# Batch-2 loads and weight stores ordered behind the raw weight loads on SyncE, and two weight conversions moved between softmax sums, in a fused attention and cos-FFN kernel

## The chip, the cores and the metric

The kernel runs on one core of one Trainium2 chip. The metric is the time of one execution on the device in microseconds (us); less is better. Before the change three runs took 944.4, 944.38 and 940.06 us, median 944.38.

## What is computed

Attention with two kinds of masks, followed by a feed-forward layer whose activation is h·cos(h). All inputs are float32.

```
def _attn_ref(q, k, v):                      # (8, 8, 576, 64): batch, heads, positions, head size
    scores = scale * np.matmul(q, k.transpose(0, 1, 3, 2))
    mask_local = (rel >= 0) & (rel < 32)                     # heads 0 to 3
    mask_strided = (rel >= 0) & (pos[None, :] % 32 == pos[:, None] % 32)   # heads 4 to 7
    attn = softmax(np.where(masks, scores, -1e9))
    return np.matmul(attn, v)

def _moe_ref(x, w_in, w_out):                # x (4608, 512), w_in (512, 2048), w_out (2048, 512)
    h = x @ w_in
    g = h * np.cos(h)
    return g @ w_out
```

## The kernel before

The 4608 tokens are worked through in 12 blocks `j` of 384. The hidden width of 2048 is cut into 16 slices `f` of 128. A **chunk** (j, f) is `hidden`: 12 matmuls of 384 columns into PSUM bank a or b (L467), the curve h·cos(h) on ACT and DVE (L473, L474, L477, L480), and a split of the result into a high part on ACT (L483) and a rest on POOL (L484). `outer` follows three chunks later (`LAG`): 9 matmuls of 512 columns into the output's accumulators (L491). High and low parts exist because each float32 operand is multiplied in two parts.

Blocks 0 to 5 (`PLAIN`) are done in this way, blocks 6 to 11 in pairs by a scheme with seven products for eight (L757 and L786), which reads sums and copies of the weights back from DRAM, `wis` and `wos`.

Attention is cut into seven **units** a batch: four strided ones (L360 for scores) and three local ones (L305). A unit is: scores on PE; a softmax that goes back and forth between DVE (maximum L249, subtraction L250, sum L272, L273, reciprocal L274), ACT (exponent L261) and POOL (product L276); then either three transposes on PE (L380, strided) or one on DVE (L314, local); the products with v (L394 or L329); and a copy to x by ACT. The 14 units of batches 0 and 1 come ahead of the feed-forward ("plain"), with an Exp; the 42 units of batches 2 to 7 lie between the chunks of blocks 2 to 5, with two Silu and a Square (L265, L266, L270) in place of Exp, a subtraction on POOL (L256), and ACT's copy L384 between the transposes L380 and the products. The curve's Sin needs another table on ACT than Exp, so the first L477 has a table load ahead of it.

The **weights** come as float64 in memory. `load_weight` (L140 and below) loads one raw tile of 512 KB on SP's queue (L144; three buffers) and converts it to float32 parts: on DVE L158 (or on ACT L153, for `w_out`), L161 and L167, on ACT L166 and the cast L171, on POOL the rest L172. `need_weights` (L176) does this for `w_in` and `w_out` of slice f. A converted slice's first DVE operation is ordered behind the curve's L474 of chunk (0, f - 2): `after = reduced[f - AHEAD]`. For f = 0 and 1 there is no such order, and they are converted among the softmaxes of batches 0 and 1; f = 2 and up follow among the chunks. Raw tile number n is ordered behind load number 4 + n of the attention's q and k.

`put_away` (L584) stores parts of the converted weights to `wis` (L589) and `wos` (L597), also on SP's queue. The later units' loads of q and k (L295, L345) and of v (L291, L349) stand on the same queue.

The program text gives no final order: a scheduler puts each engine's instructions in an order by a simulated time, kept within the explicit `order(later, first, ...)` calls. Each engine and each queue then works strictly in that order.

Of the kernel before, what the change touches and what calls it, by code (L numbers as in the profile page):

```python
# [13 lines left out]
F32 = mybir.dt.float32  # L14
# [5 lines left out]
ALU = mybir.AluOpType  # L20
AX = mybir.AxisListType

B, H, S, D = 8, 8, 576, 64
# [22 lines left out]
VL = (LU + 1) * D  # L46
QS, KS, VS = SU * GB, SU * GB, SU * D
# [7 lines left out]

LAG = 3
AHEAD = 2

WEIGHTS_AT, WEIGHTS_EACH = 4, 1

# [26 lines left out]
def attention_cos_ffn(ctx, tc, qkl, vl, qkvs, w_in, w_out, eye, eye16, mask_l0, mask_l, mask_s, out):  # L87
    nc = tc.nc
# [21 lines left out]
    pn_s = [const.tile([P, SU, GP], F32, name=f"pn_s{i}") for i in range(2)]  # L110
    for t in pn_s:
        nc.gpsimd.memset(t, 0.0)
    exps, reduced, loads, tiles = [], [], [], []

    def half(n, rows=64):
        return slice(64 * n, 64 * n + rows)
# [4 lines left out]
    def order(later, first, reason):  # L121
        tc.add_manual_dep(
            later.ins, first.ins.name,
            mybir.DependencyInfo(mybir.DependencyClass.NoSync, mybir.DependencyReason.DATA), reason=reason,
        )
# [11 lines left out]
    wis = [dram.tile([7, P, 2, 2 * P], F32, name=f"wis{q}") for q in range(NQ)]  # L137
    wos = [dram.tile([P, 2, DM], F32, name=f"wos{f}") for f in range(NFC)]
# [35 lines left out]
    weights = 0  # L174

    def need_weights(cv, f):  # L176
        nonlocal weights
        for f in range(weights, f + 1):
            after = reduced[f - AHEAD] if 0 <= f - AHEAD < len(reduced) else None
            load_weight(  # L180
                cv, w_in.bitcast(I32)[f], wi_h[f].rearrange("p c n -> p (c n)"),
                wi_l[f].rearrange("p c n -> p (c n)"), after, False,
            )
            load_weight(cv, w_out.bitcast(I32)[f], wo_h[f], wo_l[f], after, True)
            weights = f + 1
# [16 lines left out]
    class Attention:  # L202
# [42 lines left out]
        def softmax(self, s, mask, n, w, pn=None):  # L245
            t = self.wk.tile([P, SC], F32, name="t_sb", bufs=3 if self.plain else 2)[:, :n * w].rearrange("p (t w) -> p t w", w=w)
            mx = sm.tile([P, SU], F32, name="mx")
            if self.plain:
                nc.vector.tensor_reduce(out=mx[:, :n], in_=s, op=ALU.max, axis=AX.X)  # L249
                nc.vector.tensor_tensor(  # L250
                    out=t, in0=s, in1=mx[:, :n].unsqueeze(2).broadcast_to([P, n, w]), op=ALU.subtract
                )
            else:
                nc.vector.tensor_tensor(out=t, in0=s, in1=mask, op=ALU.add)
                nc.vector.tensor_reduce(out=mx[:, :n], in_=t, op=ALU.max, axis=AX.X)
                nc.gpsimd.tensor_tensor(  # L256
                    out=t, in0=t, in1=mx[:, :n].unsqueeze(2).broadcast_to([P, n, w]), op=ALU.subtract
                )
            if self.plain:
                e = t  # L260
                exps.append(nc.scalar.activation(out=e, in_=t, func=AF.Exp, scale=0.125))  # L261
            else:
                e = self.wk.tile([P, SC], F32, name="e_sb", bufs=3)
                e = e[:, :n * w].rearrange("p (t w) -> p t w", w=w)
                nc.scalar.activation(out=e, in_=t, func=AF.Silu, bias=shift1, scale=0.0625)  # L265
                nc.scalar.activation(out=t, in_=t, func=AF.Silu, bias=shift2, scale=0.0625)  # L266
                nc.vector.scalar_tensor_tensor(
                    out=e, in0=t, scalar=-math.exp(STEP), in1=e, op0=ALU.mult, op1=ALU.add
                )
                nc.scalar.activation(out=e, in_=e, func=AF.Square, scale=math.exp(SHIFT) / STEP)  # L270
            z = sm.tile([P, SU], F32, name="z")
            nc.vector.tensor_reduce(out=z[:, :n], in_=e, op=ALU.add, axis=AX.X)  # L272
            nc.vector.tensor_scalar(out=z[:, :n], in0=z[:, :n], scalar1=1e-9, scalar2=None, op0=ALU.add)  # L273
            nc.vector.reciprocal(out=z[:, :n], in_=z[:, :n])  # L274
            pn = e if pn is None else pn
            nc.gpsimd.tensor_tensor(  # L276
                out=pn, in0=e, in1=z[:, :n].unsqueeze(2).broadcast_to([P, n, w]), op=ALU.mult
            )
            return pn
# [7 lines left out]
        def local(self, b, u):  # L287

            def load_v():
                v = self.ld.tile([P, max(VL, VS)], F32, name="v", bufs=5 if self.plain else 3)  # L290
                nc.sync.dma_start(out=v[:, :VL], in_=vl[b, u])  # L291
                return v

            qk = self.ld.tile([P, max(QKL, QS + KS)], F32, name="qk")
            loads.append(nc.sync.dma_start(out=qk[:, :QKL], in_=qkl[b, u]))  # L295
            if self.plain:
                v = load_v()
            q_t = qk[:, :2 * LQ].rearrange("p (h q) -> p h q", h=2)
            k_t = qk[:, 2 * LQ:QKL].rearrange("p (h k) -> p h k", h=2)
            mask = ml0.rearrange("p (t w) -> p t w", w=KW) if u == 0 else ml.unsqueeze(1).broadcast_to([P, LU, KW])  # L300
            s_ps = self.score_bank(mask)

            def score(t, c):
                p, j = divmod(c, 2)
                self.scored = self.pe(nc.tensor.matmul(  # L305
                    s_ps[quarter_of(c), t * KW:(t + 1) * KW], q_t[half(j), p, QB * t:QB * (t + 1)],
                    k_t[half(j), p, QB * t:QB * t + KW], start=not self.plain, stop=True, skip_group_check=True,
                ))

            yield [partial(score, t, c) for t in range(LU) for c in range(LH)], "64x32"  # L310
            pn = self.softmax(s_ps[:, :LU * KW].rearrange("p (t w) -> p t w", w=KW), mask, LU, KW)

            pt = self.wk.tile([P, LU * KW], F32, name="pt_l", bufs=2 if self.plain else 3)
            nc.vector.transpose(out=pt[:, :LU * KW], in_=pn.rearrange("p t w -> p (t w)"))  # L314
            yield
            if not self.plain:
                v = load_v()
            v_t = v[:, :VL].rearrange("p (m d) -> p m d", d=D)
            yield
            x_t = [self.wk.tile([P, LQ], F32, name="x_l") for _ in range(2)]  # L320
            a_ps = [self.bank(self.products), self.bank(self.transposed)]

            def product(m, c):


                p, j = divmod(c, 2)
                lo, hi = max(m - 1, 0), min(m + 1, LU)
                at = m * KW - QB if m else 0
                self.pe(nc.tensor.matmul(  # L329
                    a_ps[p][half(j), lo * QB:hi * QB], v_t[quarter_of(c), m], pt[quarter_of(c), at:at + (hi - lo) * QB],  # L330
                    start=m == turns[0], stop=m == turns[-1], skip_group_check=True,
                ))


            turns = range(0 if u else 1, LU + 1)
            yield [partial(product, m, c) for m in turns for c in range(LH)], "32x64"
            nc.scalar.copy(out=x_t[0], in_=a_ps[0][:, :LQ])
            nc.scalar.copy(out=x_t[1], in_=a_ps[1][:, :LQ])
            for p in range(2):
                keep(2 + p, b * S + u * LQ, x_t[p])  # L340

        def strided(self, b, p, u):
            real = min(SU, NG - SU * u)
            qk = self.ld.tile([P, max(QKL, QS + KS)], F32, name="qk")
            loads.append(nc.sync.dma_start(out=qk[:, :QS + KS], in_=qkvs[b, p, u, :, :QS + KS]))  # L345

            def load_v():
                v = self.ld.tile([P, max(VL, VS)], F32, name="v", bufs=5 if self.plain else 3)
                nc.sync.dma_start(out=v[:, :real * D], in_=qkvs[b, p, u, :, QS + KS:QS + KS + real * D])  # L349
                return v  # L350

            if self.plain:
                v = load_v()
# [21 lines left out]
            if not self.plain:  # L375
                v = load_v()
# [29 lines left out]
            if full < real:  # L406
                left = STRIDE % GR
                nc.scalar.copy(
                    out=x_v[:, :, STRIDE - left:],
# [173 lines left out]

    def put_away():  # L584

        for q in range(NQ):
            for i, f, k in ((1, q, 0), (2, q, 1), (5, q + NQ, 1)):
                for part, w in enumerate((wi_h, wi_l)):
                    nc.sync.dma_start(  # L589
                        out=wis[q][i][:, part],  # L590
                        in_=w[f][:, 2 * k:2 * k + 2].bitcast(F32).rearrange("p c n -> p (c n)"),
                    )
                if i != 2:
                    yield
            for f in (q, q + NQ):
                for part, w in enumerate((wo_h, wo_l)):
                    nc.sync.dma_start(out=wos[f][:, part], in_=w[f].bitcast(F32))  # L597
                yield

    direct = {j: x_operands() for j in range(2)}  # L600
# [349 lines left out]
```

## Time and profile before

| | |
|---|---|
| three timed runs | 944.4, 944.38, 940.06 us |
| profiled execution | 939.62 us, its span 937.8 us |
| PE busy | 903.8 us, 96% of the span |
| DVE, ACT, POOL busy | 527.8, 519.8, 436.4 us |
| PE idle from 45 to 60, 60 to 80 us | 5.54, 2.16 us |
| PE idle from 80 to 260 us | 0 us |
| PE idle from 260 to 500 us | 14.8 us |
| DMA moved | 166.33 MB, mean 177 GB/s |

The span is the time from the first to the last instruction; the execution's time has 1.8 us around it. The units of batches 0 and 1 end, and the chunks begin, near 55 us; batch 2 begins near 200 us, the paired blocks near 500 us. PE's busy time by itself says little, since a matmul's end is modelled and overlaps the next one's start; where consecutive matmuls start at steady distances (0.174 us for 384 columns, 0.229 us for 512) PE is full.

In the quoted rows of a timeline the columns are the start and the duration in us, the engine, line, operation, the output and its inputs, the shapes, how many instructions in a row are merged, and in brackets the idle time ahead of it on this engine and what ended it. Rows of waits give the total, the number of times and the longest in us.

### The profile page before, as it was taken

Reading aid. Unit: us, or ns where it says so; the run is one execution under the profiler, and the core shown is the slowest. Engines: PE = TensorE matmul, PEld = TensorE weight load, DVE = VectorE, ACT = ScalarE, POOL = GpSimd, SP = SyncE. Lnnn points to the kernel's source line nnn. Section 1 sums busy time; section 2 is a strip of 40 time slices with the busy share of each in tenths; the row PEclk is TensorE's granted clock in tenths of the full one; section 3 lists DMA queues with packets and bytes.
Section 4 is the critical chain, followed back from the end, with each engine's and each line's share of the span. In section 5 each row is a group of like instructions: output and inputs, shape, how many; then the busy total and the mean of one; then the engine's idle time right before and its main releaser. Section 6 shows DMA issues by size and latency. Waiting matters only on the chain.

```text
span 937.8 us, 20557 instructions
## 1 busy us (share of the span) xinstructions
PE 903.8 (96%) x7876; PEld 793.2 (85%) x7876; DVE 527.8 (56%) x1018; ACT 519.8 (55%) x1090; POOL 436.4 (47%) x466
## 2 busy tenths in 40 slices
PE   8879999999999997999999999999999999999998
PEld 4668899998888886888878889898998889999996
DVE  5758756446657555665654334646456464545453
ACT  3556777466666555665565544545555455544443
POOL 2636665535655566555745522535325444223231
PEclk9799999999999999999999999999999999999999
DMA  8938866222245534544354856666676565756401
GB/s 287 317 116 290 281 227 215 94 100 86 92 154 184 172 120 155 172 148 129 121 203 135 273 159 190 202 195 202 199 247 215 185 196 162 253 186 208 136 23 67
DMA packets 93265, 166.33 MB, mean 177 GB/s; under 512 B 10736, under 2 KB 34032, under 8 KB 93168
## 3 DMA queue, kind: packets, MB, share of 16 engines
q1 hardware_dynamic: 85248, 157.72, 52.0%
q10 hardware_dynamic: 7920, 7.31, 2.3%
q8 instruction: 62, 1.02, 0.5%
q14 instruction: 35, 0.29, 0.1%
HBM read 125.40 MB, written 39.58 MB: 176 GB/s over the span
## 4 chain that ended last, share of the span: by engine, by line
PE 43%; POOL 10%; DVE 7%; ACT 7%; issue 5%; DMA 1%; ACTq 0%; POOLq 0%; DVEq 0%
PE acc L786 18%; PE a L757 10%; PE b L757 7%; PE acc L491 4%; POOL g_lo L484 3%; POOL t_sb L256 2%; PE b L467 2%; PE a L467 2%; POOL wf L559 2%; POOL sr L567 1%; DVE r L480 1%; ACT e_sb L265 1%; DVE r L766 1%; DVE r L768 1%; POOL pn_s L276 1%
## 5 line engine op out<-in xcount | busy, mean ns | idle before, releaser
L772 POOL TENSOR_TENSOR g_lo<-r,g_hi 128x384 fp32r<-128x384 f32 x96 | 101.9, 1061 | 246.2 <-ACT g_hi L771 141.3
L484 POOL TENSOR_TENSOR g_lo<-r,g_hi 128x384 fp32r<-128x384 f32 x96 | 102.8, 1070 | 167.9 <-ACT g_hi L483 96.0
L491 PE MATMUL acc<-s,g_hi 128*128 128x512 f32 x576 | 180.0, 396 | 0.0
L786 PE MATMUL acc<-s,g_hi 128*128 128x512 f32 x576 | 179.7, 393 | 0.0
L491 PEld LDWEIGHTS acc<-s,g_hi 128*128 128x128 f32 x576 | 105.3, 188 | 15.5
L786 PEld LDWEIGHTS acc<-s,g_hi 128*128 128x128 f32 x576 | 106.2, 188 | 10.8
L786 PE MATMUL acc<-s,g_lo 128*128 128x512 f32 x288 | 112.8, 392 | 0.0
L766 DVE SCALAR_TENSOR_TENSOR r<-r,h 128x384 f32<-128x384 int32 x96 | 64.0, 667 | 85.5 <-ACT r L765 85.5
L491 PE MATMUL acc<-s,g_lo 128*128 128x512 f32 x288 | 110.9, 390 | 0.0
L467 PE MATMUL b<-x_hi,s 128*128 128x384 f32 x384 | 109.5, 346 | 1.1 <-DVE r L480 1.1
L467 PE MATMUL a<-x_hi,s 128*128 128x384 f32 x384 | 109.5, 346 | 1.0 <-DVE r L480 1.0
L757 PE MATMUL a<-s,s 128*128 128x384 f32 x384 | 83.1, 337 | 0.0
L767 ACT ACTIVATE r<-r,biases 128x384 f32<-128x384 f32 x96 | 59.2, 617 | 42.5 <-DVE r L766 42.4
L768 DVE TENSOR_TENSOR r<-r,h 128x384 f32<-128x384 f32 x96 | 64.5, 671 | 23.6 <-ACT r L767 21.6
L477 ACT ACTIVATE r<-r,biases 128x384 f32<-128x384 f32 x96 | 58.9, 614 | 30.8 <-DVE r L474 29.1
L765 ACT ACTIVATE r<-h 128x384 int32<-128x384 f32 x96 | 50.3, 524 | 45.0 <-DVE h L835 29.4
L467 PEld LDWEIGHTS b<-x_hi,s 128*128 128x128 f32 x384 | 71.0, 190 | 4.6 <-DVE r L480 1.9
L467 PEld LDWEIGHTS a<-x_hi,s 128*128 128x128 f32 x384 | 70.6, 189 | 4.0 <-DVE r L480 1.4
L757 PEld LDWEIGHTS a<-s,s 128*128 128x128 f32 x384 | 69.3, 188 | 4.2
L771 ACT CAST g_hi<-r 128x384 fp32r<-128x384 f32 x96 | 49.1, 512 | 42.0 <-DVE r L768 41.9
L483 ACT CAST g_hi<-r 128x384 fp32r<-128x384 f32 x96 | 49.0, 511 | 34.6 <-DVE r L480 33.7
L467 PE MATMUL b<-x_lo,s 128*128 128x384 f32 x192 | 64.8, 338 | 0.0
(141 smaller groups left out, 1764.6 us busy)
## 6 DMA issues: line engine op xcount, KB each, us to landing
s<-wis SPq DMA_DIRECT2D x168, 256.0 KB, 2.9
s<-wos SPq DMA_DIRECT2D x96, 256.0 KB, 3.5
qk<-in_qkvs SPq DMA_DIRECT2D x32, 324.0 KB, 3.6
qk<-in_qkl SPq DMA_DIRECT2D x24, 416.0 KB, 3.9
out<-o SPq DMA_DIRECT2D x36, 256.0 KB, 2.6
raw<-in_w_in SPq DMA_DIRECT2D x16, 512.0 KB, 5.4
raw<-in_w_out SPq DMA_DIRECT2D x16, 512.0 KB, 3.9
wos<-s SPq DMA_DIRECT2D x32, 256.0 KB, 5.1
```

Of the source, the lines that this page charges most:

```text
L467: mm = nc.tensor.matmul(h, w[f][:, c], x[c], start=(i == 0), stop=(i == len(ops) - 1))
L477: sin = nc.scalar.activation(out=r, in_=r, func=AF.Sin, bias=quarter)
L484: chain["rest"] = nc.gpsimd.tensor_tensor(out=g_lo, in0=r, in1=g_hi.bitcast(F32), op=ALU.subtract)
L491: mm = nc.tensor.matmul(acc[t], g[:, ts], w[f], start=(f == 0 and i == 0), stop=(f == NFC - 1 and i == 2))
L757: in_turn(nc.tensor.matmul(bank, w[:, n, c], part, start=start and i == 0, stop=stop and i == len(ops) - 1, skip_group_check=True,))
L765: nc.scalar.activation(out=k, in_=h, func=AF.Copy, scale=1.0 / (2.0 * math.pi), bias=0.25)
L766: nc.vector.scalar_tensor_tensor(out=r, in0=k, scalar=-2.0 * math.pi, in1=h, op0=ALU.mult, op1=ALU.add)
L767: nc.scalar.activation(out=r, in_=r, func=AF.Sin, bias=quarter)
L768: chain["curve"] = nc.vector.tensor_tensor(out=r, in0=r, in1=h, op=ALU.mult)
L771: chain["cast"] = nc.scalar.copy(out=g_hi, in_=r)
L772: chain["rest"] = nc.gpsimd.tensor_tensor(out=g_lo, in0=r, in1=g_hi.bitcast(F32), op=ALU.subtract)
L786: in_turn(nc.tensor.matmul(acc, g[gn][:, ts], w[wn], start=done == 0 and i == 0, stop=done == NFC - 1 and i == 2,))
```

## The change

Three things are done.

- All loads of units that are not plain (batches 2 to 7) are ordered behind the last raw load, `tiles[-1]`.
- All stores of `put_away` are ordered behind the last unit load that the program has named at that point, `loads[-1]`. So they too stand behind the raw loads.
- Slices f = 2 and 3 are converted behind the softmax sum (L272) number 10 and 13 of the plain units, counted from 0, in place of the curves of chunks (0, 0) and (0, 1). Sums 10 and 13 belong to the eleventh and the last of the 14 plain units.

```diff
 LAG = 3
 AHEAD = 2
+CONVERTED = {2: 10, 3: 13}
...
-            after = reduced[f - AHEAD] if 0 <= f - AHEAD < len(reduced) else None
+            after = summed[CONVERTED[f]] if f in CONVERTED else reduced[f - AHEAD] if f >= AHEAD else None
...
-            nc.vector.tensor_reduce(out=z[:, :n], in_=e, op=ALU.add, axis=AX.X)
+            summed.append(nc.vector.tensor_reduce(out=z[:, :n], in_=e, op=ALU.add, axis=AX.X))
...
             loads.append(nc.sync.dma_start(out=qk[:, :QKL], in_=qkl[b, u]))
+            if not self.plain:
+                order(loads[-1], tiles[-1], "weights first")
...
-                nc.sync.dma_start(out=v[:, :VL], in_=vl[b, u])
+                load = nc.sync.dma_start(out=v[:, :VL], in_=vl[b, u])
+                if not self.plain:
+                    order(load, tiles[-1], "weights first")
...
+        def put(out, part):
+            order(nc.sync.dma_start(out=out, in_=part), loads[-1], "units first")
+
         for q in range(NQ):
...
-                    nc.sync.dma_start(
-                        out=wis[q][i][:, part],
-                        in_=w[f][:, 2 * k:2 * k + 2].bitcast(F32).rearrange("p c n -> p (c n)"),
-                    )
+                    put(wis[q][i][:, part], w[f][:, 2 * k:2 * k + 2].bitcast(F32).rearrange("p c n -> p (c n)"))
...
-                    nc.sync.dma_start(out=wos[f][:, part], in_=w[f].bitcast(F32))
+                    put(wos[f][:, part], w[f].bitcast(F32))
```

No instruction is added or taken away on an engine. In the changed file the lines are numbered one to nine higher (L158 is L159 there, L161 L162, L167 L168, L172 L173, L249 L250, L272 L273, L274 L275, L384 L393, L473 L482).

**DVE and POOL at the end of the plain units.** On DVE, from the sum of unit 10 to the sum of unit 11; before:

```order
L272 TENSOR_REDUCE z<-t_sb 128x6
L273 TENSOR_SCALAR z<-z 128x6
L274 RECIPROCAL z<-z 128x6
L249 TENSOR_REDUCE mx<-acc_851 128x6
L250 TENSOR_TENSOR t_sb<-acc_851,mx 128x324
L272 TENSOR_REDUCE z<-t_sb 128x6
```

and in the changed kernel, where `bits` and `raw` are the tiles of a weight's conversion:

```order
L273 TENSOR_REDUCE z<-t_sb 128x6
L159 TENSOR_SCALAR bits<-raw 128x512
L274 TENSOR_SCALAR z<-z 128x6
L162 SCALAR_TENSOR_TENSOR bits<-raw,bits 128x512
L162 SCALAR_TENSOR_TENSOR bits<-raw,bits 128x512
L275 RECIPROCAL z<-z 128x6
L250 TENSOR_REDUCE mx<-acc_851 128x6
L168 SCALAR_TENSOR_TENSOR bits<-raw,bits 128x512
L251 TENSOR_TENSOR t_sb<-acc_851,mx 128x324
L168 SCALAR_TENSOR_TENSOR bits<-raw,bits 128x512
L273 TENSOR_REDUCE z<-t_sb 128x6
```

The five DVE operations of f = 2 stand between the steps of two softmaxes; the same five of f = 3 stand in the same manner around the last unit's reciprocal. On POOL, from the product of unit 10 (`pn_s_85`) to that of unit 12, the changed kernel has

```order
L277 TENSOR_TENSOR pn_s_85<-t_sb,z 128x6x54
L173 TENSOR_TENSOR s_142<-bits,s_126 128x512
L173 TENSOR_TENSOR s_110<-bits,s_94 128x512
L277 TENSOR_TENSOR pn_s_86<-t_sb,z 128x6x54
L435 TENSOR_TENSOR x_lo<-x_l,x_hi 128x192 x2
L277 TENSOR_TENSOR t_sb<-t_sb,z 128x384
```

where before the two rests of the weights, now ahead of unit 11's product `pn_s_86`, stood behind the first chunk's L484.

**SP's queue.** Behind the raw load of `w_out` for f = 1, before:

```order
L144 DMA raw<-in_w_out 128x1024
L291 DMA v<-in_vl 128x448
L589 DMA wis_160<-s_92 128x256 x2
L291 DMA v<-in_vl 128x448
L345 DMA qk<-in_qkvs 128x648
L589 DMA wis_160<-s_108 128x256
L144 DMA raw<-in_w_in 128x1024
L589 DMA wis_160<-s_108 128x256
L597 DMA wos_168<-s_124 128x512
```

In the changed kernel those stores are gone from there and the first of them stand behind the last raw load, between the first loads of batch 2:

```order
L145 DMA raw<-in_w_out 128x1024
L350 DMA qk<-in_qkvs 128x648
L596 DMA wis_160<-s_92 128x256
L596 DMA wis_160<-s_108 128x256
L350 DMA qk<-in_qkvs 128x648
```

**ACT among the later units.** The scheduler also gave ACT, DVE and POOL another order at a number of places from batch 2 on, with PE's order there unchanged. One of them on ACT, before, around the copy `pt<-acc_3103`:

```order
L473 ACTIVATE r<-b 128x384
L265 ACTIVATE e_sb<-t_sb,biases 128x384
L384 COPY pt<-acc_3103 128x324
L266 ACTIVATE t_sb<-t_sb,biases 128x384
L477 ACTIVATE r<-r,biases 128x384
```

and in the changed kernel:

```order
L266 ACTIVATE e_sb<-t_sb,biases 128x384
L267 ACTIVATE t_sb<-t_sb,biases 128x384
L482 ACTIVATE r<-b 128x384
L393 COPY pt<-acc_3103 128x324
L271 ACTIVATE e_sb<-e_sb 128x384
L486 ACTIVATE r<-r,biases 128x384
```

The copy now stands behind both Silu of the next unit's softmax and the chunk's L473.

More of the change, by code (lines that the diff above doesn't have):

```diff
@@ L112, in attention_cos_ffn @@
         nc.gpsimd.memset(t, 0.0)
-    exps, reduced, loads, tiles = [], [], [], []
+    exps, summed, reduced, loads, tiles = [], [], [], [], []
     def half(n, rows=64):
@@ L345, in strided @@
             loads.append(nc.sync.dma_start(out=qk[:, :QS + KS], in_=qkvs[b, p, u, :, :QS + KS]))
+            if not self.plain:
+                order(loads[-1], tiles[-1], "weights first")
             def load_v():
                 v = self.ld.tile([P, max(VL, VS)], F32, name="v", bufs=5 if self.plain else 3)
-                nc.sync.dma_start(out=v[:, :real * D], in_=qkvs[b, p, u, :, QS + KS:QS + KS + real * D])
+                load = nc.sync.dma_start(out=v[:, :real * D], in_=qkvs[b, p, u, :, QS + KS:QS + KS + real * D])
+                if not self.plain:
+                    order(load, tiles[-1], "weights first")
                 return v
```

## The prediction, made blind

> **What bounds the kernel now.** I read the page's span first, then a table of busy time by stretches of the span, because the share of 96% for PE is an average over very different stages.
>
> ```profile
> span 937.8 us, 20557 instructions
> core 0: us, PE busy (x) PEld busy (x) DVE busy (x) ACT busy (x) POOL busy (x), PEclk, DMA share, GB/s
> 18.00:45.00 27.00, 22.95 (x525) 17.19 (x524) 20.97 (x48) 15.84 (x43) 18.81 (x22) 0.75 0.96 319
> 45.00:60.00 15.00, 9.46 (x310) 7.65 (x299) 7.79 (x21) 6.38 (x21) 5.33 (x8) 0.98 0.20 65
> 60.00:80.00 20.00, 17.84 (x85) 16.05 (x84) 14.85 (x22) 13.99 (x26) 9.14 (x7) 0.93 0.78 250
> 80.00:180.00 100.00, 100.00 (x505) 90.82 (x504) 62.34 (x107) 70.87 (x132) 59.45 (x49) 1.00 0.67 223
> 180.00:260.00 80.00, 80.00 (x868) 70.62 (x867) 46.56 (x102) 48.76 (x104) 42.05 (x50) 1.00 0.30 97
> 260.00:500.00 240.00, 225.21 (x3110) 195.48 (x3109) 146.22 (x329) 141.32 (x327) 139.99 (x174) 0.99 0.47 152
> ```
>
> From 80 to 260 us PE is never idle: 100.00 of 100 and 80.00 of 80. Most of the stores that the change moves, and the DMA queues that are 0.67 busy there, cost PE nothing in that stretch. PE has something to lose or to win in three places only: ahead of 45 us (clock 0.75, DMA 0.96), from 45 to 80 (5.5 and 2.2 us idle), and from 260 to 500 (14.8 us idle). The list of what PE waited for after 60 us is headed by the third.
>
> ```profile
> PE acc L329 <- ACT pt L384: 9.2, 5, 2.8
> PE acc L380 <- ACT x_l L338: 5.2, 4, 2.2
> ```
>
> No row of that list names a DMA. The other waits of weight in it are two on r, of 1.0 and 1.1 us, whose rows stand further down; it is only through these that a late raw load of weights reaches PE.
>
> **Conversion of f = 2 and 3, moved ahead.** Prices first, from the timeline of DVE and POOL where f = 2 is converted now:
>
> ```profile
> 62.82 0.42 DVE L158 TENSOR_SCALAR bits<-raw 128x512 int32<-128x512 int32 x1
> 63.15 1.29 DVE L161 SCALAR_TENSOR_TENSOR bits<-raw,bits 128x512 int32<-128x512 int32 x2
> 66.47 0.69 DVE L167 SCALAR_TENSOR_TENSOR bits<-raw,bits 128x512 int32<-128x512 int32 x1
> 68.00 2.56 POOL L172 TENSOR_TENSOR s<-bits,s 128x512 fp32r<-128x512 f32 x2
> ```
>
> One f is 0.42 + 1.29 + 2 x 0.64 = 3.0 us of DVE and 2.56 us of POOL. These now stand inside the softmax chains of the last four units of batch 1, where each step waits for the one ahead:
>
> ```profile
> 49.11 0.73 POOL L276 TENSOR_TENSOR pn_s<-t_sb,z 128x324 f32<-128x324 f32 x1 [1.08 <-DVE z L274]
> 52.04 0.83 POOL L276 TENSOR_TENSOR t_sb<-t_sb,z 128x384 f32<-128x384 f32 x1 [1.10 <-DVE z L274]
> 53.41 0.52 DVE L249 TENSOR_REDUCE mx<-b 128x6 f32<-128x384 f32 x1
> 57.34 0.58 DVE L314 STREAM_TRANSPOSE pt_l<-t_sb 128x384 f32<-128x384 f32 x1 [1.19 <-POOL t_sb L276]
> 58.33 1.02 PE L329 MATMUL acc<-pt_l,v 32*64 32x32 f32 x56 [2.65 <-DVE pt_l L314]
> ```
>
> Unit 10's reciprocal gets L158 and two L161 ahead of it, 1.7 us. On POOL both L172 of f = 2 stand ahead of unit 11's pn_s (49.11). They wait for ACT's two casts, the second of which waits for the second L167; adding the durations up I get the casts done at about 51.1, pn_s at 52.5, and after it the two x_lo of POOL's row, so that unit 12's product (52.04) starts at about 54.35, 2.3 late. Its transpose, and behind it on DVE unit 13's maximum (53.41), are as late. Unit 13's own reciprocal then gets f = 3's L158 and two L161 ahead of it, 1.7 more; its two L167 lie in the wait for POOL (1.19). So the last L329 comes about 4.0 us later than 58.33.
>
> That is without waits between DVE and POOL, and the trace shows such waits earlier, where the same operations ran beside POOL:
>
> ```profile
> 19.91 1.27 POOL L172 TENSOR_TENSOR s<-bits,s 128x512 fp32r<-128x512 f32 x1
> 20.51 1.23 DVE L167 SCALAR_TENSOR_TENSOR bits<-raw,bits 128x512 int32<-128x512 int32 x1
> 23.10 1.26 POOL L172 TENSOR_TENSOR s<-bits,s 128x512 fp32r<-128x512 f32 x1
> 23.40 1.25 DVE L158 TENSOR_SCALAR bits<-raw 128x512 int32<-128x512 int32 x1
> ```
>
> L158 takes 1.25 us there and 0.42 alone; L167 1.23 and 0.64; both end about when POOL's operation does. Two such meetings add 0.6 + 0.8 = 1.4 us, so the last L329 is 4.0 to 5.4 us late. [...]
>
> What comes back is behind that L329:
>
> ```profile
> 59.37 0.32 ACT L337 COPY x_l<-acc 128x192 f32<-128x192 f32 x1 [2.89 <-PE acc L329]
> 59.72 0.81 ACTq L459 DMA_DIRECT2D xT<-x_l  x2
> 61.82 0.49 ACT L473 ACTIVATE r<-a 128x384 int32<-128x384 f32 x1 [1.91 <-PE a L467]
> 62.90 1.28 ACT L477 ACT_TABLE_LOAD   x1
> 64.19 0.62 ACT L477 ACTIVATE r<-r,biases 128x384 f32<-128x384 f32 x1
> 65.45 0.44 PE L467 MATMUL a<-x_hi,s 128*128 128x384 f32 x1 [1.04 <-DVE r L480]
> 71.85 0.68 ACT L153 ACTIVATE bits<-raw 128x512 int32<-128x512 uint32 x1 [1.97 <-DMA raw<-in_w_out]
> 79.31 0.44 PE L467 MATMUL b<-x_hi,s 128*128 128x384 f32 x1 [1.12 <-DVE r L480]
> ```
>
> Now 6.1 us pass from the end of L329 (58.33 + 1.02) to the third chunk's start (65.45), and on ACT an L153 (0.68, as at 71.85) stands between L473 and the table load. In the changed order PE does the whole first chunk of L467 and three matmuls of the second ahead of L329, so ACT's L473 can follow the two copies at once: copies 0.5, L473 0.5, two DMA issues 0.8, table load 1.3, L477 0.6, L480 0.55, starts 0.15: 4.4 us, with no L153 between. That is 1.7 us back. From 65.45 to 79.31 are 13.9 us; the 36 matmuls of 384 columns (starts 0.174 apart in this stretch) and 27 of 512 (0.229) need 12.4. The difference of 1.4 goes, because f = 3, whose L153 sat on ACT's queue for 1.97 us until its raw tile landed, is done by then. Sum: +4.0 - 1.7 - 1.4 = **+0.9 us** without the waits at POOL, +2.3 with them; I take the middle, **+1.6**. The bounds: if f = 2 hides wholly in the idle time of that stretch, only f = 3's 1.7 is left and 1.7 - 3.1 = -1.4; if another stretch of half clock falls behind the longer gap ahead of L329 and into dense work, it costs half of some 3.4 us more, +2.3 + 1.7 = +4. The profile has one such stretch behind the gap of 2.65 us; it is what brings the clock from 60 to 80 us to 0.93 (7% of 20 us lost is 1.4, near that half of 3.4). [...]
>
> **Loads and stores on SP.** Removed from 18 to 180 us: 80 stores of weights, now behind the last raw load.
>
> ```profile
> q1 hardware_dynamic: 85248, 157.72, 52.0%
> wos<-s SPq DMA_DIRECT2D x32, 256.0 KB, 5.1
> wis<-s SPq DMA_DIRECT2D x48, 128.0 KB, 4.9
> qk<-in_qkvs SPq DMA_DIRECT2D x32, 324.0 KB, 3.6
> ```
>
> They are 14.7 MB, by q1's row 14.7 / 157.72 x 52% x 937.8 = 45 us of all 16 engines. Between 180 and 300 us they raise a share of 0.30 to about 0.7. SP spends 0.33 us on each issue, and waits most of its time there anyway. Unit loads stand among them with two buffers, some 11 us ahead of their use against 3.6 us to landing; even 5.1 fits. I take **0**; with the cover gone, a load late by 1.5 us at one unit in eight of 42 costs +8. Ahead of 45 us the relief can help: PE stalled at 23.58 without a releaser, the clock then fell, and slow matmuls stand ahead of DVE's wait at 39.87.
>
> ```profile
> 23.58 0.49 PE L305 MATMUL a<-qk 64*32 64x64 f32 x18 [1.71 <-issue]
> 34.97 3.19 PE L329 MATMUL acc<-pt_l,v 32*64 32x32 f32 x100 [1.17 <-ACT x_t L402]
> ```
>
> At full clock the 100 matmuls and the six behind them take 2 us less. Bounds -2 and 0; I take 0, since DVE is busy without a pause up to 35 us and keeps its order.
>
> **Order on ACT, 240 to 500 us.** The scheduler put the two L265/L266 of the next softmax ahead of the copy L384 at five places (at 241, 271, 292, 372 and 394 us). What this does is seen where it is so already:
>
> ```profile
> 364.16 0.61 ACT L265 ACTIVATE e_sb<-t_sb,biases 128x384 f32<-128x384 f32 x1 [3.79 <-POOL t_sb L256]
> 365.70 0.42 ACT L384 COPY pt<-acc 128x324 f32<-128x324 f32 x1
> 366.17 1.37 PE L329 MATMUL acc<-pt_l,v 32*64 32x32 f32 x52 [2.82 <-ACT pt L384]
> ```
>
> ACT stood still for 3.79 us for POOL with L384 queued behind. Of ten copies in that order now, four made PE wait. Five more, each later by L266 and L473 (0.5 + 0.4), give 0 to +4.5; two places go the other way, -2 if they heal waits. I take **+2.0**.
>
> **Sum.** +1.6 + 0 + 2.0 = +3.6 us on the profiled execution's 939.62 (span 937.8 and 1.8 around it): 943.2. The four executions shown (939.62, 940.06, 944.38, 944.4) have their middle at 942.2, 2.6 above the profiled one; so **945.8 us**.
>
> **Rivals.** (1) *DMA relief decides.* The stall at 23.58 goes, the clock stays up (-2), f = 2 hides (-1.4 in place of +1.6), and no copy gets later (0 in place of +2): 945.8 - 7 = 938.8. For it: a DMA share of 0.96 in the very stretch where stores leave. Against it: no row shows DVE, which sets the pace there, waiting for a load or a store. (2) *ACT's head of queue decides, slower.* At all five places ACT comes to L265 before POOL is ready and PE waits 1.9 us each (9.2 / 5), 9.5 in place of 2.0: 953.3 us; with late unit loads behind the stores up to 955. It decides from the point at which POOL's L256 ends more than the 0.9 us after L384's input. For it: POOL is the one whom ACT waits for at 364. Against it: six of ten such copies cost nothing. (3) *The stores and raw loads were never in each other's way* and the conversion is a wash: 942.2 to 944.4, no change.
>
> **How the numbers follow.** Chances: forecast 0.47, rival 1 0.25, rival 2 0.19, rival 3 0.09. A measurement of this kernel can tell about 0.5% (4.7 us) from no change. Faster by more: 0.19 of rival 1 and 0.03 of the forecast's edge, 0.22. Slower by more: all of rival 2 and 0.07 of the forecast, 0.26. Within: 0.52. The range reaches from 937 (rival 1 and a spread of 2) to 955 (rival 2).
>
> **What would show it.** In the changed profile: the last L329 ahead of the first curve near 62 to 64 us; the first L480 some 3.8 us after it; no wait near 79 us, and PE full from about 70 us. Between 180 and 300 us a DMA share near 0.7 with no PE wait on a DMA. From 260 to 500 one or two more waits on L384. I am wrong if the sixth chunk starts ahead of 79 us, if PE's clock stays at 1.00 from 25 to 39 us, or if PE's idle time from 260 to 500 changes by over 5 us.

## The result, and the profile after

| | before | after |
|---|---|---|
| timed runs | 944.4, 944.38, 940.06, 941.98 | 953.51, 953.87, 952.84, 954.27 |
| median, us | 943.18 | 953.69 |
| ratio, 95% interval | 1 | 1.0116 [1.0087, 1.0145] |
| profiled execution, us | 939.62 | 953.51 |

The kernel became 1.2% slower: 10.5 us between the medians, 13.9 us between the two profiled executions. The time lies inside the predicted range (937 to 955). But I had called "no change" the likeliest, at 945.8, and the loss is three times the +3.6 of my sum.

Stretches of the changed kernel, with the columns of the table before (busy time and instructions of PE, its weight loads, DVE, ACT and POOL; the granted clock; the DMA share; GB/s):

```profile
span 951.7 us, 20514 instructions
25.00:39.00 14.00, 9.41 (x195) 7.22 (x198) 10.56 (x26) 9.19 (x25) 11.26 (x14) 0.76 0.65 212
45.00:60.00 15.00, 10.26 (x254) 8.10 (x245) 11.89 (x27) 9.05 (x23) 6.86 (x9) 0.89 0.30 105
60.00:80.00 20.00, 13.89 (x101) 12.53 (x100) 6.55 (x12) 9.45 (x18) 7.44 (x7) 0.66 0.27 83
80.00:180.00 100.00, 100.00 (x505) 91.08 (x505) 58.46 (x108) 71.82 (x132) 56.65 (x48) 1.00 0.37 131
180.00:260.00 80.00, 80.00 (x770) 70.65 (x770) 42.47 (x93) 45.65 (x95) 36.49 (x43) 1.00 0.46 146
260.00:500.00 240.00, 223.55 (x3077) 193.83 (x3079) 140.29 (x322) 138.62 (x324) 140.00 (x175) 0.97 0.57 187
```

PE is still full from 80 to 260 us, and the DMA queues are relieved as intended (0.37 in place of 0.67 from 80 to 180). Two stretches got worse: 60 to 80 us (6.1 us idle in place of 2.2, clock 0.66 in place of 0.93) and 260 to 500 us (16.5 us idle in place of 14.8, clock 0.97 in place of 0.99). PE's waits of the changed kernel after 60 us (total, times, longest):

```profile
PE acc L334 <- ACT pt L393: 8.7, 4, 2.8
PE acc L389 <- ACT x_l L343: 7.6, 7, 2.2
PE a L476 <- DVE r L489: 3.2, 1, 3.2
PE acc L334 <- ACT s L172: 3.0, 1, 3.0
```

To place the loss I compare the start of each chunk's first curve operation (ACT, L473 before and L482 after). The 25th, the 43rd and the last such instruction, of before and then of after:

```profile
161.14 0.48 ACT L473 ACTIVATE r<-a 128x384 int32<-128x384 f32 x1
244.67 0.49 ACT L473 ACTIVATE r<-a 128x384 int32<-128x384 f32 x1 [0.22 <-PE a L467]
545.89 0.49 ACT L473 ACTIVATE r<-b 128x384 int32<-128x384 f32 x1 [1.30 <-PE b L467]
```

```profile
168.18 0.48 ACT L482 ACTIVATE r<-a 128x384 int32<-128x384 f32 x1
252.35 0.48 ACT L482 ACTIVATE r<-a 128x384 int32<-128x384 f32 x1
559.37 0.49 ACT L482 ACTIVATE r<-b 128x384 int32<-128x384 f32 x1 [1.30 <-PE b L476]
```

So there are **two steps**: +7.0 us by 161 us, and 6.4 more between about 240 and 500. Outside of them nothing is lost.

**The first step** on PE: the last plain product and the third chunk of the changed kernel (start, duration, in brackets the idle time ahead and its end). Before they stand at 58.33 and 65.45.

```profile
63.66 1.72 PE L334 MATMUL acc<-pt_l,v 32*64 32x32 f32 x56 [2.96 <-ACT s L172]
71.71 0.69 PE L476 MATMUL a<-x_hi,s 128*128 128x384 f32 x1 [3.15 <-DVE r L489]
75.72 1.54 PE L500 MATMUL acc<-s,g_hi 128*128 128x512 f32 x4
```

The product is 5.3 us late, and 0.7 us longer at half clock (1.72 us, 1.02 before). The row names ACT's cast, which ended at 63.57, but what the product reads comes from DVE's transpose. That ended at 63.41, 0.25 us ahead of the product; in e8 below, where no such cast stands there, the row names the transpose. From the product's end to the third chunk pass 6.3 us, where I had worked out 4.4. ACT's rows say why:

```profile
62.95 0.62 ACT L172 CAST s<-bits 128x512 fp32r<-128x512 f32 x1 [0.62 <-DVE bits L168]
63.47 0.31 ACT L342 COPY x_l<-acc 128x192 f32<-128x192 f32 x1
63.81 0.81 ACTq L468 DMA_DIRECT2D xT<-x_l  x2
67.92 0.32 ACT L342 COPY x_l<-acc 128x192 f32<-128x192 f32 x1 [3.92 <-DMA xT<-x_l]
69.16 1.28 ACT L486 ACT_TABLE_LOAD   x1 [0.30 <-ACT r L482]
```

The casts of f = 3 stand ahead of unit 12's copies to x_l on ACT, whose product had ended at 57.9. A unit writes a pair of x_l tiles, and the two buffers hold just one pair. So the copies' store is issued only at 63.81, and unit 13's copy waits 3.92 us for it to land. The table load, the first curve and the third chunk wait behind.

The store is also slow. It takes 4.0 us to land, and the next pair, issued at 68.31, 1.6 us. Two raw loads of 512 KB were issued just ahead of it, as soon as f = 3's last two L168 were done with their tiles (61.70 and 62.94). SP's rows, what SP waited for from 58 to 66 us, the DMA share from 63 to 66 us, and the shortest, median and longest landing of the x_l stores:

```profile
61.70 0.33 SPq L145 DMA_DIRECT2D raw<-in_w_out  x1
62.94 0.33 SPq L145 DMA_DIRECT2D raw<-in_w_in  x1
SPq L145 <- DVE bits L168: 9.5, 2, 8.7
63.00:66.00 3.00, 2.34 (x58) 2.31 (x59) 0.40 (x1) 1.00 (x3) 2.26 (x2) 0.51 0.92 283
DMA to landing us min/median/max: 1.6/2.8/4.0
```

By an estimate from these rows, a store of 1.6 us would have landed at 65.4, just as the product ended (65.38). The clock adds to it (0.51 from 63 to 77 us):

```profile
63.00:77.00 14.00, 10.19 (x81) 9.40 (x82) 2.99 (x6) 6.30 (x13) 4.27 (x4) 0.51 0.31 100
```

From 63 to 77 us PE runs at half clock, so the third chunk takes 4.0 us (71.71 to 75.72). Against 65.45 the third chunk is 6.3 late; slow matmuls behind its start (0.32 us apart in place of 0.174) add some 2.2; the wait once at 79.31 is gone (1.4): 7.1, the step.

### The profile page after: what moved, and what is told of

It reads as the page before. It is cut to its first block, busy times and chain, and to the rows that moved or that the text cites. A ratio compares the mean times of both kernels' runs of the same rounds, so it can differ in the third digit from the quotient of the medians.

```text
span 951.7 us, 20514 instructions
## 1 busy us (share of the span) xinstructions
PE 910.2 (96%) x7876; PEld 798.8 (84%) x7876; DVE 520.1 (55%) x1018; ACT 520.8 (55%) x1090; POOL 435.1 (46%) x466
## 3 DMA queue, kind: packets, MB, share of 16 engines
q8 instruction: 62, 1.02, 0.4%
## 4 chain that ended last, share of the span: by engine, by line
PE 52%; DVE 6%; ACT 5%; POOL 5%; issue 3%; DMA 1%; SPq 0%; ACTq 0%; POOLq 0%; DVEq 0%
PE acc L795 17%; PE a L766 9%; PE acc L500 7%; PE b L766 7%; PE b L476 4%; PE a L476 4%; POOL g_lo L493 2%; POOL t_sb L257 1%; PE acc L334 1%; DVE r L777 1%; DVE r L775 1%; PE acc L403 1%; ACT r L776 1%; DMA out<-o 1%; POOL sr L576 1%
## 5 line engine op out<-in xcount | busy, mean ns | idle before, releaser
L476 PE MATMUL a<-x_hi,s 128*128 128x384 f32 x384 | 112.5, 354 | 3.2 <-DVE r L489 3.2
L476 PEld LDWEIGHTS a<-x_hi,s 128*128 128x128 f32 x384 | 73.2, 196 | 6.3 <-DVE r L489 3.7
L777 DVE TENSOR_TENSOR r<-r,h 128x384 f32<-128x384 f32 x96 | 64.5, 672 | 23.6 <-ACT r L776 21.6
L476 PE MATMUL a<-x_lo,s 128*128 128x384 f32 x192 | 66.4, 346 | 0.0
```

Of the source, the lines that this page charges most:

```text
L476: mm = nc.tensor.matmul(h, w[f][:, c], x[c], start=(i == 0), stop=(i == len(ops) - 1))
L777: chain["curve"] = nc.vector.tensor_tensor(out=r, in0=r, in1=h, op=ALU.mult)
```

## The experiments

Two theories for the first step: (A) f = 3's conversion, through the order on ACT, the x_l buffers and the clock; (B) the raw loads crowd the DMA queues at 63 us and hold the x store up. Two for the second: (C) the new order on ACT that came with the change; (D) the moved stores. A "tie" is an explicit order between two instructions. Where ACT's order is tied, the tie runs along 395 instructions, PE's order stays, and the scheduler moves some DVE and POOL rows along with ACT (107 and 33 in e10, 51 and 16 in e11; in e12's rows the 256 tied steps of the softmax and the curve and copies of pt start in just the tied order); so "ACT's order" below means these together. In those kernels one helper line stands for all of ACT's tied lines.

| run | median us | ratio to before | tenth maximum | third chunk | curve 25 | last curve |
|---|---|---|---|---|---|---|
| after | 953.69 | 1.0116 [1.0087, 1.0145] | 39.93 | 71.71 | +7.0 | +13.5 |
| e1 | 951.2 | 1.0092 [1.0071, 1.0113] | 40.02 | 74.25 | +9.4 | +11.8 |
| e2 | 940.45 | 0.9983 [0.9965, 1.0001] | 40.05 | 65.25 | +0.3 | +0.7 |
| e3 | 949.95 | 1.0078 [1.0056, 1.0099] | 39.44 | 69.10 | +2.2 | +9.7 |
| e4 | 950.56 | 1.0087 [1.0063, 1.0112] | 41.09 | 71.11 | +5.7 | +11.8 |
| e5 | 942.0 | one run | 41.42 | 65.81 | +1.5 | +2.4 |
| e6 | 949.34 | 1.0079 [1.0049, 1.0109] | 40.65 | 72.79 | +8.0 | +7.5 |
| e7 | 943.87 | 1.0026 [1.0011, 1.0041] | 41.52 | 70.50 | +3.6 | +6.5 |
| e8 | 935.66 | 0.9930 [0.9906, 0.9953] | 38.86 | 66.19 | -0.8 | -5.1 |
| e9 | 941.24 | 0.9999 [0.9981, 1.0017] | 40.10 | 67.63 | +0.7 | +1.9 |
| e10 | 941.9 | 1.0017 [1.0002, 1.0032] | 39.30 | 71.21 | +5.8 | +1.7 |
| e11 | 935.07 | 0.9941 [0.9920, 0.9962] | 39.12 | 64.36 | -0.6 | -5.8 |
| e12 | 928.45 | 0.9865 [0.9836, 0.9894] | 38.77 | 63.83 | -1.2 | -12.7 |

The last four columns are of each run's one profiled execution: the start of the tenth unit's maximum on DVE (39.87 before), which lies ahead of the first moved conversion, the start of the third chunk, and by how many us the 25th and the last curve start later than in the first profile of before. That the same program differs by 1.5 and 2.4 there (e5) is the measure of what these columns can tell. At curve 25 nearly all of this scatter is there at the tenth maximum already. With that taken off, curve 25 lies within 0.1 us of before in e2, e5, e11 and e12, which convert as before, and is later by 7.0 us in after, 9.2 in e1, 2.6 in e3, 4.5 in e4, 7.3 in e6, 1.9 in e7, 0.3 in e8, 0.5 in e9 and 6.4 in e10.

### e1 to e4: which part, and where

e1 is before with the conversion alone; e2 is after with the ties alone:

```diff
-CONVERTED = {2: 10, 3: 13}
+CONVERTED = {}
```

> Before plus CONVERTED alone; loads and stores keep their old places on SP. Theory A (the first 7.0 us of the shift come from the two conversions put into the last softmaxes: a later last product, x_l copies behind casts, and a half-clock stretch behind the longer gap): last plain product at 63 to 64 us, third chunk at 71 to 72 (before 65.4), chunk curves near 130 us 6 to 8 us later than before; no more than 1.5 us of it is given back without the ties. Rival B (the raw loads, no longer held up by stores, crowd the DMA queues at 63 us and delay the x store): without ties the third chunk starts by 69, the shift at 130 us is 4 us or less. For the second step (6.5 us between 240 and 470): if the moved stores cause it, the shift stays what it is at 130 us to the end, 946 to 948 us in all; if ACT's changed order and the clock cause it, it grows by 3 to 7 us here too, 949 to 954.

> After with CONVERTED empty: only the ties on SP. Theory A: third chunk at 65 to 66 us as before, shift near 130 us within 1 us of nothing. Rival B: shift at 130 us of 3 us or more. For the second step: if the moved stores load the DMA queues so that x stores land late and ACT waits, the shift grows by 5 to 7 us between 240 and 470 us and the time is 948 to 951 us; if it is ACT's order and where idle gaps fall in the clock's 3.4 us windows, PE idle from 260 to 500 stays within 2 us of 14.8 and the shift is that of the extra half-clock time, somewhere between -2 and +6.

The 3.4 us of e2's second step is what the granted clock shows in the two profiles. Behind 55 us the half clock lasts from 59.42 to 62.84 and from 366.62 to 370.04 in the first profile of before, and from 63.04 to 76.69, 274.67 to 278.08, 377.07 to 383.89 and 435.09 to 438.51 in that of after: 3.41 us or two or four times as long, and within a profile the starts lie whole multiples of 3.41 us apart.

The ties alone change nothing that can be measured, neither in 60 to 80 us nor behind 240 us, although the moved stores are all there: D falls, and so does B as far as the ties would cause it. What B describes happens all the same, but through the conversion, which sets the raw loads of 61.70 and 62.94 free. The conversion alone carries the loss, and the new order on ACT comes with it: by the traces e1's differs from that of before in 73 instructions, those of the moved conversions among them, and e2's in 7. In e1 the first step is larger, without the ties (third chunk at 74.25); my bound of 1.5 us for that was a miss. In that profile the x_l copy waited 5.0 us for its store in place of 3.9, among weight stores that the ties take away from there (DMA share 0.62 from 60 to 80 us, in place of 0.27).

e3 gives the plain units four x_l buffers, with no instruction reordered; e4 puts the two casts of f = 3 behind unit 12's copies:

```diff
-            x_t = [self.wk.tile([P, LQ], F32, name="x_l") for _ in range(2)]
+            x_t = [self.wk.tile([P, LQ], F32, name="x_l", bufs=4 if self.plain else 2) for _ in range(2)]
```

```diff
-        nc.scalar.copy(out=hi, in_=w)
+        cast = nc.scalar.copy(out=hi, in_=w)
+        if len(tiles) in (7, 8):
+            order(cast, copies[4], "x of the unit before first")
```

> After with four x_l buffers in place of two for the plain units, the same order of instructions. Theory A with the buffer in it: the 3.9 us wait of the last unit's x_l copy for the store of the unit before is gone; third chunk at 68 to 69 us instead of 71.7, shift near 130 us of +3 to +4.5 instead of +7.0, time 2.5 to 4 us below the changed kernel. If the clock stretch from 63 to 76.7 us stays, the gain is at the lower end. Rival (the clock alone sets it, the gap length does not matter): the shift stays above +6.

> After with the two casts of f = 3 ordered behind the x_l copies of the unit before the last on ACT; nothing else moves on any engine. Theory A: the copies run 1.5 to 3 us earlier (60.5 to 62 us instead of 63.5), so their store has landed by 65 or 66 and the third chunk starts at 69 to 70; shift near 130 us of +4.5 to +6. Rival (the store is slow because raw loads fill the DMA queues, not because it is issued late): its landing stays near 67.5 and the shift at +6.5 or more.

With four buffers the wait is gone, and the first step falls from 7.0 to 2.2. PE's rows in e3:

```profile
63.55 1.72 PE L334 MATMUL acc<-pt_l,v 32*64 32x32 f32 x56 [2.17 <-ACT s L172]
69.10 0.44 PE L476 MATMUL a<-x_hi,s 128*128 128x384 f32 x1 [1.30 <-DVE r L489]
71.29 1.54 PE L500 MATMUL acc<-s,g_hi 128*128 128x512 f32 x6
```

The product comes as late as in the changed kernel, but the third chunk 2.6 us sooner and at full clock (2.2 us in place of 4.0). The gain is larger than those 2.6 us, since the half clock ends at 67 us in place of 77. The third chunk runs at half clock, wholly or in part, in all five profiles with this wait (after, e1, e4, e6, e10), and in neither of the two with four buffers (e3, e7). e4 moved the store's issue only from 63.81 to 63.32 where I had expected 60.5 to 62, and the third chunk only to 71.11: the two L167 of f = 3 stand ahead of the copies as well, and they stayed there. But this execution was 1.2 us late at the tenth maximum. Counted from there the store is issued 1.7 us sooner than in the changed kernel and has landed 1.8 us sooner, and curve 25 is 4.5 us late in place of 7.0: what theory A had expected. The store still took 3.9 us, beside the same two raw loads, and the copy waited 1.8 us.

### e5 to e7: how much is chance, and ACT's order

e5 is before once more. e6 is after with ACT's order from about 235 to 515 us tied to that of before, and e7 has the four buffers as well:

```diff
+    for name in PIN:
+        op = acts[name][at[name]]
+        at[name] += 1
+        if last is not None:
+            order(op, last, "ACT as before")
+        last = op
```

> The kernel before, unchanged, profiled once more. If the stretches of half clock between 260 and 500 us are set by the program alone, they come at 366 us again, 3.4 us in all, and PE busy from 260 to 500 us stays at 225 us, the execution at 938 to 941. If they depend on where the clock's 3.4 us grid happens to lie under the same idle gaps, this execution has another count of them (two to four in 260 to 500) and differs by about 1.5 us for each; then part of the second step of the shift (6.5 us in the one pair of profiles) is chance, and the difference of the medians, 10.5 us, is the one to explain.

> After with ACT's 395 instructions from about 235 to 515 us tied in the order that they have in the kernel before; the conversions and the ties on SP stay. If ACT's changed order makes the second step (x_l and pt copies later, PE idle from 260 to 500 us 16.5 in place of 14.8 us or less), PE's idle time there falls to 11 to 15 us, the shift grows by no more than 3 us between 240 and 500, and the time is 3 to 5 us below the changed kernel: 948 to 950. If it is the clock's stretches or the moved stores, the order changes nothing: growth of 5 to 7 us, 952 to 954.

> Both edits, four x_l buffers and ACT's order of before from 235 us on. If the two steps are what I take them for, they add: shift near 130 us of +2 to +3.5, to the end +2 to +6, time 943 to 947, no more than 0.5% above before. If the second step is not ACT's order, as with four x_l buffers alone: 949 to 951.

The same program had one stretch of half clock between 260 and 500 us in its first profile, from 366.62 to 370.04, and in e5 one where the first has none. The window from 260 to 280 us, first profile and then e5:

```profile
260.00:280.00 20.00, 18.29 (x265) 15.84 (x264) 10.77 (x24) 11.63 (x28) 10.61 (x15) 1.00 0.45 143
```

```profile
260.00:280.00 20.00, 18.32 (x246) 15.89 (x248) 10.11 (x24) 11.71 (x29) 10.59 (x14) 0.91 0.45 138
```

Equal idle time (1.7 us), other clock (1.00 and 0.91): part of the 13.9 us between the two profiles is chance, and the 10.5 between the medians is what has to be explained. In e6 the second step is gone (+8.0, then +7.5). PE's waits from 260 to 500 us in e6 (L350 is the product, L405 the transpose):

```profile
PE acc L350 <- ACT pt L127: 7.5, 4, 2.8
PE acc L405 <- ACT x_l L127: 5.2, 4, 2.2
```

The waits on x_l are back at the 5.2 us of before, from 7.6. The intervals of after and e6 overlap, though, so these two runs alone don't separate the 3.5 us; e9 to e11 do it better. e7 adds both edits and lands at 1.0026: from e6 to e7 the buffers are worth 0.53%, 5 us. Its profile, at 946.43 us, lies above its median, so its columns show more than the 2.4 us that are left by the ratio.

### e8 to e12: f = 2 alone, and orders exchanged

e8 moves only f = 2 (`CONVERTED = {2: 10}`).

> After with only f = 2 moved; f = 3 stays behind the curve of chunk (0, 1), as before. By the working of the prediction f = 2 costs 2.3 us at the last plain product (60.6 in place of 58.3 us) or up to 3.1 with waits at POOL, and the 1.4 us at 79 us are not won back. If the casts of f = 3 in front of the x_l copies are what makes the x store late, that wait is gone or under 1 us here, the third chunk starts at 67 to 68.5 us, and the shift near 130 us is +2 to +3.5. If f = 2 alone delays the x store as well, third chunk at 70 or later and +5 or more.

It came out 0.7% faster than before, below every number that I had written. PE's rows at the same two places:

```profile
60.66 1.02 PE L334 MATMUL acc<-pt_l,v 32*64 32x32 f32 x56 [1.72 <-DVE pt_l L319]
66.19 0.44 PE L476 MATMUL a<-x_hi,s 128*128 128x384 f32 x1 [1.01 <-DVE r L489]
```

This execution was 1.0 us early at the tenth maximum. Counted from there the product is 3.3 us late, 4.5 us lie between its end and the third chunk in place of 6.1, and the wait at 79 us is gone: +0.3 in sum. But 4.3 of the 5.1 us won come between 240 and 500 us, where this kernel has yet another order on ACT. So the orders were exchanged: e9 is e8 with the order of before, e10 is after with the order of e8, e11 is before, without any part of the change, with the order of e8. The edit is that of e6 with another list.

> Only f = 2 moved, the ties on SP, and ACT's 395 instructions from about 235 to 515 us in the order of the kernel before. If the gain of f = 2 alone (6 us) is 0.8 us of conversion and the rest ACT's order by chance, the rest goes: shift near 130 us about -0.8, to the end -2 to +2, time 939 to 943, ratio to before 0.998 to 1.001. If the moved conversion itself is worth 6 us, it stays at 935 to 937.

> After with those 395 instructions in the order that they have in the run with only f = 2 moved. If order decides, PE's idle time from 260 to 500 us is 8 to 11 us in place of 16.5 and the shift falls by 3 to 5 us between 240 and 500: +7 near 130 us, +2 to +4 at the end, 944 to 947. If that run's second gain came from elsewhere, the shift stays at +7 or grows, 949 to 954.

> Before, without any part of the change, with the same ACT order. If order decides, it is 3 to 5 us faster than before: 937 to 939, PE idle from 260 to 500 us 8 to 11 us. If the order needs the change's timing around it, no difference: 941 to 943.

The order takes its gain along wherever it goes: 0.9930 becomes 0.9999 without it, 1.0116 becomes 1.0017 with it, and before itself becomes 0.9941. And the conversion costs the same under either order: e6 is 0.8% over before, e10 0.8% over e11. I had expected less of the order: e10, e11 and e12 came out 1.5 to 2.1 us below the times that I gave.

What the good order has is seen in its rows: at several places it puts the curve's first step and the copy of pt ahead of the next softmax's Silu. e12 carries this on to the nine places where one or both Silu still stood ahead of both (five, with one Silu between the two, stay as they are), in before without any part of the change (a and b are the two Silu, k the curve's first step, f the copy of pt):

```diff
-... jjabkfclm ... jjakfblcm ...
+... jjkfabclm ... jjkfablcm ...
```

> Before, no part of the change, with the ACT order of e11 in which moreover the curve's first step and the copy of pt stand ahead of both Silu at the nine places where that order still had one or both Silu ahead of them. If the head of ACT's queue (a Silu that waits for POOL) makes the waits of the products on the copy of pt, those waits, 6.9 us in e11, fall below 3 us and the time falls by 2 to 5 us more: 930 to 934. If the copies are late for another reason (PE's own transposes, POOL's product), the waits move to x_l or stay, and the time is that of e11, 934 to 937, or longer because the softmaxes start later.

928.45 us, 1.35% faster than before, the best of all. PE's waits from 260 to 500 us in e11 and then in e12, and ACT in e12 at the place that I had quoted from before at 364 us:

```profile
PE acc L345 <- ACT pt L126: 6.9, 4, 2.8
PE acc L396 <- ACT x_l L126: 3.2, 4, 1.3
```

```profile
PE acc L396 <- ACT x_l L126: 5.1, 5, 2.3
```

```profile
354.53 0.49 ACT L126 ACTIVATE r<-a 128x384 int32<-128x384 f32 x1 [0.67 <-PE acc L396]
354.92 0.42 ACT L126 COPY pt<-acc 128x324 f32<-128x324 f32 x1
357.67 0.61 ACT L126 ACTIVATE e_sb<-t_sb,biases 128x384 f32<-128x384 f32 x1 [2.33 <-POOL t_sb L272]
```

The copy now runs while ACT would stand still for POOL, and no wait on pt is left; 1.9 us of the gain went into x_l. PE is busy for 234.68 of the 240 us, at full clock throughout:

```profile
260.00:500.00 240.00, 234.68 (x3233) 202.77 (x3235) 150.30 (x338) 149.28 (x343) 145.99 (x180) 1.00 0.51 161
```

## Why the prediction was right or wrong

**Conversion, +1.6 forecast: measured +7.4** (e6 against before, 0.79%; e10 against e11, 0.76%; both with the ties, which by e2 are worth nothing), beyond my upper bound of 4. The pieces:
- The last product was forecast 4.0 to 5.4 us late; it was 5.3. The dearer end, with the operations of DVE that run long beside POOL's, was right; f = 2 has 3.3 of it (e8), where the sum without meetings had 2.3. The long operations that I quoted for such meetings don't end about when POOL's do, as I wrote, but 0.6 and 0.3 us after it (21.74 against 21.18, 24.65 against 24.36), about the time that they take alone (0.64 and 0.42). DVE's and one of POOL's rows in the changed kernel at f = 3:

```profile
59.32 1.69 DVE L162 SCALAR_TENSOR_TENSOR bits<-raw,bits 128x512 int32<-128x512 int32 x2
61.03 1.88 DVE L168 SCALAR_TENSOR_TENSOR bits<-raw,bits 128x512 int32<-128x512 int32 x2
62.84 0.57 DVE L319 STREAM_TRANSPOSE pt_l<-t_sb 128x384 f32<-128x384 f32 x1
61.25 1.11 POOL L277 TENSOR_TENSOR t_sb<-t_sb,z 128x384 f32<-128x384 f32 x1 [0.79 <-DVE z L275]
```

  The pair of L168 takes 1.88 us beside POOL in place of 1.28, POOL's product 1.11 in place of 0.83, and the transpose starts right behind it: it doesn't "lie in the wait for POOL", as I wrote.
- The step that failed is "ACT's L473 can follow the two copies at once", the 1.7 us back. I summed durations behind the product and didn't ask what the first copy itself waits for. It writes one of two buffers whose last reader is a DMA. ACT issues that DMA behind the very casts that the change puts there, and it then takes 4.0 us in place of 1.6, beside the raw loads that the end of f = 3's conversion sets free. The lateness and the slowness weren't tried apart. Without that wait (e3) the piece from product to third chunk is 3.8 us, even below my 4.4, and the step is +2.2, close to the 2.3 of my dearer sum. With it came the clock.
- The half clock: I had priced one more stretch at 1.7, an estimate from the one in the profile of before (59.42 to 62.84, behind 2.65 us of idle time). It lasted 13.7 us instead (63.04 to 76.69), over two gaps of PE, and covered the third chunk. That length is of this one execution: in e6 and e10 the clock from 60 to 80 us is 0.83, 6.8 us of half clock. The trace shows what the estimate lacked: on the 3.4 us grid of these drops (63.0, 66.5, 69.9, 73.3) each of the first three windows holds idle time of PE (busy for 82, 62 and 46%), the fourth none, and the clock is back at its end, 76.7; in e3 the first window, from 63.5, is busy for 99% already, and the clock is back at 66.9. Idle time in a window doesn't always prolong it, though: in e10 PE was busy for 83% of the window from 64.5, and the clock came back at its end.
- The 1.4 us at 79 us came back as forecast, with f = 2 alone already (e8, e9), where I had put it down to f = 3; with the ties alone (e2) that wait is still there.
- f = 2 alone is worth nothing either way (e9: 0.9999 [0.9981, 1.0017]); by the same terms the forecast for it is 2.3 - 1.7 - 1.4 = -0.8. So the loss comes with f = 3, which wasn't run without f = 2.

**Loads and stores, 0 forecast: right** (e2). No PE wait on a DMA appeared. The DMA share from 180 to 300 us is 0.48, not the 0.7 that I had estimated: the stores spread over a longer stretch, with 0.57 in place of 0.47 from 260 to 500. The clock stayed up longer from 25 to 39 us (0.76, where the first profile has 0.51), and it bought nothing that can be seen: DVE's maximum stands at 39.87 before and at 39.93 after. Nor need the relief have raised it, since e11, whose loads and stores are those of before, shows 0.76 at a DMA share of 1.00. The maximum of after and the stretch of e11:

```profile
39.93 0.56 DVE L250 TENSOR_REDUCE mx<-a 128x6 f32<-128x384 f32 x1 [4.25 <-PE a L310]
25.00:39.00 14.00, 9.41 (x236) 7.62 (x236) 9.80 (x25) 9.29 (x28) 10.84 (x13) 0.76 1.00 351
```

**ACT's order, +2.0 forecast: measured +3.5** (1.0116 against 1.0079, with overlapping intervals), inside my bounds of -2 to 4.5. The direction and the root were right: copies that stand behind a Silu. The place was partly wrong. I looked for more waits on the copy of pt, and these went from 9.2 to 8.7; the waits on x_l rose from 5.2 to 7.6, and the half clock there is four times 3.4 us (3.4 from 274.7, 6.8 from 377.1, 3.4 from 435.1) in place of one in the first profile of before, each worth up to 1.7 by the estimate at the end. Rival 2, with 9.5 us for the same root, was too dear. But the root is worth more than that the other way: e12, which heals the order, wins 11.5 us between the 25th and the last curve.

7.4 and 3.5 make 10.9 us, the 1.16% of 943; they do so by construction, since 3.5 is what e6 leaves of the whole. **The chances** failed with the first term: I bounded it by what the rows of DVE and PE allowed, and left out the buffers. That the time lies inside the range is luck: the range reaches to 955 for rival 2, whose 9.5 us did not come, and a loss that I had not foreseen filled the place. My signs of being wrong didn't catch it either: none of the three came, though the first L489 followed the last product by 7.4 us (71.10) where I had named 3.8.

Open: why the scheduler's order on ACT differs behind 235 us with a change made at 50 us. I saw that it does, that it comes with the conversions and what it costs, not by which simulated times. And how much of an order's worth lies in the DVE and POOL rows that move with ACT wasn't tried apart.

## What to carry to other kernels

Where work is put into another engine's queue, follow every instruction behind it one step further, to the buffer it writes and the DMA that must have read it: a double buffer is cover only as long as the store is issued and lands on time (here a copy waited 3.92 us for a store of 4.0). In a strict queue a short instruction that another engine waits for belongs ahead of one that itself waits (e12, 1.35%). And when a scheduler decides the order, a small edit redraws it everywhere: pin the order when an edit is measured, or the order's luck (here -0.6 to +0.4%) is booked to the edit.

## What was unexpected of the hardware

The half clock isn't the same in two executions of one program with the same gaps: between 260 and 280 us e5 has a granted clock of 0.91, so by estimate a drop of some 3.4 us, the first profile 1.00. Laid on the grid of 3.4 us that a profile's drops show, PE's (modelled) busy share of a window tells most of it: in nine profiles (before, after, e1, e6, e7 and e9 to e12), from 55 to 930 us, each of the 28 drops follows a window in which PE was busy for 58% or less, and no window below 44% was followed by one at full clock. A drop in dense work costs up to 1.7 us, an estimate: half of 3.4 us, since matmuls of 384 columns start 0.32 us apart at half clock (after, 72 to 75 us) and 0.174 at full. The runs of the kernel before lay between 937.3 and 945.0 us; another part of that scatter is the start, where the tenth maximum lies between 38.8 and 41.5 us over the profiles. The drop isn't a fixed price either: 3.4 us where the next window was busy throughout (after, from 274.67), 13.7 us where three windows in a row held idle time (after, from 63.04). With five waits left on PE between 80 and 500 us, e12 had no drop from 80 us to its last 2 us (clock 1.00).
